# FFT mixing and a maxout FFN on one core: the first batch's start reordered, the stage-one pieces of later batches regrouped, and the last stores spread over three queues

## The chip, the cores and the metric

The kernel runs on one NeuronCore of one Trainium2 chip. The core has a matrix engine (TensorE; PE in the profile, PEld for its weight loads), three engines for elementwise work (VectorE, here DVE; ScalarE, ACT; GpSimd, POOL), and SyncE (SP), which here only starts transfers. ACT and POOL start transfers too; an engine's name with a q behind it (SPq, ACTq, POOLq) is the sequencer of that engine starting one. Time is microseconds (us) of one execution on the device; the time of a kernel is the median of its runs.

## The reference

The input x has 8 batches of 3072 tokens with 256 features. Each batch goes through a two-dimensional Fourier transform, of which the real part is kept, and then through a feed-forward layer that takes the largest of three products:

```python
X = np.fft.fft(x, axis=1)
X = np.fft.fft(X, axis=2)
t = X.real.reshape(8 * 3072, 256)
h = np.maximum(np.maximum(t @ w1, t @ w2), t @ w3)      # 256 -> 768
out = h @ w_out                                         # 768 -> 256
```

The weights are float32 in memory; the output is float32 of 24576 x 256.

## The kernel before, in words

**The algebra.** Because x is real, tokens k and 3072 - k of a batch are the sum and the difference of an even part tE and an odd part tO, so only 1536 columns of each are computed. The feature transform is folded into the weights: gE, gO and gD are products of the cosine and sine tables md and nmd with differences of the weights (w2 - w1 and w3 - w1), gw is the linear part through w_out. The maximum then is a ReLU of one difference (stmp, on ACT) and a maximum with the other (hp for token k, hm for its mirror token, on DVE).

**The token transform of a batch** (class `Mix`) is done in pieces, each a method with a letter:

- `s(0)` to `s(6)`: stage one. Two matmuls of the input xt with a small table `tab` go to the two halves of a PSUM tile; ACT (sometimes DVE) casts the result into the tile tb. `s(6)` is a small one, for the last row (line 374; the others are line 369).
- `y`: two stores of a part of tb to a scratch buffer db in memory (line 383). `z` loads db back transposed, as yb (line 390). Both are on SP's queue.
- `u`: POOL copies one column of xt to x0u (line 394). `x0`: two small matmuls on x0u (line 399); ACT casts the result to x0s (line 401). `c`: ACT copies x0s into a column of yb (line 404).
- `k(which, g)`: stage two. For a group g of 512 columns, six or so small matmuls of yb with the tables te_tab (which = 0, giving tE) or to_tab (which = 1, giving tO), line 411, and a cast out of PSUM, line 413. `k(1, g)` needs what `c` wrote; `k(0, g)` does not.

**The main loop** runs over 8 batches x 18 units: three blocks of 512 columns, and in each six slices jc of 128 of the 768 hidden features. `begin(g)` multiplies tE and tO with gE and gO (lines 436 and 437, or 771 and 772) and makes hp; `finish(g)`, one unit later, adds the product with gD (line 444) and makes hm. Every other unit from the seventh on is "split": POOL makes the sums plus and minus for it (line 764) from an even part (DVE, line 760) and an odd part (ACT, line 759). The second layer of a block (`l2_block`, lines 475, 483 and 460) is a generator of which ten steps are taken per unit of the following block. DVE writes its output tile ot (line 488), one half is stored by SP's queue (line 496), the other by an indirect store of POOL (line 570). The pool of ot has 6 buffers, the PSUM pool `ps_f` 3; the latter is shared by all the pieces above.

**What sets the order.** Every engine issues its instructions in the order in which the program text emits them. The pieces of the next batch are placed at units of the current one by tables: `ahead0` for what is done during batch 0, `ahead` during batches 1 to 6. A unit's pieces come after its `begin`, `finish` and ten second-layer steps. `turn` (line 129) puts ACT copies for the batch after next at units 5 to 12.

**The start.** For batch 0 all of this has to be done before the loop begins, on tables that are made at the same time: `table(0)`, `table(1)` and `table(2)` are three ACT instructions (te_tab, an absolute value, to_tab; lines 279, 281 and 283), called for the columns 0 to 512, and then for 512 to 1024, which only group g = 1 uses. `product` and `keep_product` make the first half of gE, gO and gD (PE line 296; casts in lines 306 and 308, line 309 for gD). `warm_up(n)` issues n matmuls on zeros (line 588) whose result nobody reads.

**The end.** The second layer of the last block is `l2_last`. It takes the four sub-blocks in the order 3, 0, 1, 2; each leaves its output tile through plain stores, six for the first and four for each of the others (line 531). For sub-block 2 the two halves of ot are copied out of PSUM separately (line 521), for the others in one copy (line 523).

Of the kernel before, what the change touches and what calls it, by code (L numbers as in the profile page):

```python
# [28 lines left out]
def _runs(slot):  # L29

    if slot == 11:
        return [(0, 48, 0), (48, 96, 16), (96, 128, 15 + 32 * 64)]
    t, u = divmod(slot, 3)
    edge, r = 96 - 32 * u, 4 * t + 1 + u
    return [(0, edge, r + 32 * 32 * u), (edge, 128, r + 1)]
# [15 lines left out]
def kernel(  # L51
# [9 lines left out]
    nc = tc.nc  # L61
# [78 lines left out]
    ps_s = ps_s_cm.__enter__()  # L140
# [86 lines left out]
    dve = nc.vector.tensor_copy  # L227
    half = gen.tile([128, 256], FP32, tag="half")
# [47 lines left out]
    def table(k, c0=1024, c1=NHALF + 1):  # L276
        cs = slice(c0, c1)
        if k == 0:
            nc.scalar.activation(out=te_tab[:, cs], in_=kvec[:, cs], func=AX.Sin, scale=step)
        elif k == 1:  # L280
            nc.scalar.activation(out=q[:, cs], in_=kvec[:, cs], func=AX.Abs)
        else:
            nc.scalar.activation(out=to_tab[:, cs], in_=q[:, cs], func=AX.Sin, scale=-step,
                                 bias=half_pi)

    def tables(c0, c1):
        for k in range(3):
            table(k, c0, c1)

    def product(i, half, jh, pool, tag):  # L290

        psg = pool.tile([128, 512], FP32, name="psg", tag=tag)
        hs = slice(half * 128, (half + 1) * 128)
        for k, (table, wt) in enumerate(((md, (w2_bf, w3_bf)[i]), (nmd, w1_bf))):
            for fc in range(2):
                nc.tensor.matmul(
                    psg[:, 0:384], table[fc][:, hs],
                    wt[:, fc * DFF + jh * 384: fc * DFF + jh * 384 + 384],
                    start=(k == 0 and fc == 0), stop=(k == 1 and fc == 1))
        return psg  # L300

    def keep_product(psg, i, half, jh, evict_e):

        cs = slice(jh * 384, (jh + 1) * 384)
        if half == 0:
            evict_e(out=gE[i][:, cs], in_=psg[:, 0:384])
        else:
            nc.scalar.copy(out=gO[i][:, cs], in_=psg[:, 0:384])
            nc.vector.tensor_scalar(out=gD[i][:, cs], in0=gO[i][:, cs], scalar1=dif,
                                    scalar2=None, op0=ALU.mult)  # L310
# [142 lines left out]
    def stored(st, mine, others):  # L453
        for group in others:
            tc.declare_no_dep(st.ins, group=group, reason="each store has rows of its own")
        tc.add_to_no_dep_group(mine, st.ins)

    def l2_hidden(po, hcols):
        for jc in range(NJC):
            nc.tensor.matmul(po, hcols(jc), wout_bf[:, jc * 256:(jc + 1) * 256],  # L460
                             start=False, stop=(jc == NJC - 1), skip_group_check=True)
            yield
# [36 lines left out]
    def l2_last(hp, hm, te, to, flipped):  # L499

        base = (B - 1) * S
        ter, tor = flipped
        for sub in (3, 0, 1, 2):
            slot = 8 + sub
            cp = slice(slot * 128, slot * 128 + 128)
            sp = slice(sub * 128, sub * 128 + 128)
            sm = slice((3 - sub) * 128, (4 - sub) * 128)
            ot = out_pool.tile([128, 512], FP32, name="ot", tag="ot")
            for (h, tev, tov, wo, hid) in (
                    (0, te[:, cp], to[:, cp], gw[:, 256:512], lambda jc: hp[:, jc, sp]),  # L510
                    (1, ter[:, sm], tor[:, sm], gw[:, 512:768], lambda jc: hm[:, jc, sm])):
                if h == 0 or sub == 2:
                    po = ps_o.tile([128, 512], FP32, name="po", tag="po")
                ph = po[:, h * 256:(h + 1) * 256]
                nc.tensor.matmul(ph, tev, gw[:, 0:256], start=True, stop=False)
                yield
                nc.tensor.matmul(ph, tov, wo, start=False, stop=True)
                yield
                yield from l2_hidden(ph, hid)
                if sub == 2:  # L520
                    nc.vector.tensor_copy(out=ot[:, h * 256:(h + 1) * 256], in_=ph)
            if sub != 2:
                nc.vector.tensor_copy(out=ot, in_=po)
            stores = [(p0, p1, base + k0, 0) for (p0, p1, k0) in _runs(slot)]
            for (p0, p1, k0) in _runs(slot):
                if k0 == 0:
                    p0, k0 = 1, 32
                stores.append((128 - p1, 128 - p0, base + S - k0 - 32 * (p1 - p0 - 1), 256))
            for k, (p0, p1, row, c) in enumerate(stores):
                eng = (nc.sync, nc.scalar)[k % 2]  # L530
                stored(eng.dma_start(out=out[row: row + 32 * (p1 - p0 - 1) + 1: 32, :],
                                     in_=ot[p0:p1, c:c + 256]), "direct", ("scattered",))

# [52 lines left out]
    def warm_up(n):  # L586
        for _ in range(n):
            nc.tensor.matmul(warm, zero[:, 0:128], zero, start=True, stop=True)
# [7 lines left out]
    m = Mix(0)  # L596
# [28 lines left out]
                                in_=moe_w_out.rearrange("(jc p) c -> p jc c", jc=NJC))  # L625
    for half in range(2):
        keep_product(product(0, half, 0, ps_f, "ps"), 0, half, 0, dve)
    for half in range(2):
        keep_product(product(1, half, 0, ps_s, "ps"), 1, half, 0, dve)
    tables(512, 1024)  # L630
    warm_up(6)
    m.c(0, 6, nc.scalar.copy)
    m.k(0, 0, dve)
    m.k(1, 0)

    rows_v = rows_f.rearrange("p (b r) -> p b r", r=12)
    adj = gen.tile([128, 12], FP32, tag="adj")
# [82 lines left out]
    for b in range(2, B):  # L720
# [3 lines left out]
        for ch in range(8):  # L724
# [1 line left out]
        at(b - 2, 13 + 3 * (b == 2), lambda b=b: mirror_first(b))  # L726

    ahead0 = {5: ("s0", "s1"), 6: ("s2", "y0", "s3"), 7: ("s4", "s5", "s6", "y1", "u"),
              8: ("z", "x"), 12: ("c",), 13: ("kO0",), 14: ("v0", "kE0", "kO1"),
              15: ("v1", "kE1"), 16: ("kO2",), 17: ("v2", "kE2", "end")}  # L730
    ahead = {1: ("s0", "s1"), 2: ("s2", "y0", "s3"), 3: ("u", "s4", "s5"), 4: ("s6", "y1", "x"),
             7: ("z",), 11: ("c",), 12: ("kO0",), 13: ("v0", "kE0", "kO1"), 14: ("v1", "kE1"),
             15: ("kO2",), 16: ("v2", "kE2", "end")}
    for b in range(B - 1):
# [56 lines left out]
    for g in range(B * UNITS):  # L791
        b, u = divmod(g, UNITS)
# [30 lines left out]
        if jc == NJC - 1:  # L823
            l2_some(1000)
            if g == B * UNITS - 1:
                finish(*prev)
            l2_queue.append(l2_last(hp, hm, mm.tE, mm.tO, flipped) if last else
                            l2_block(b, blk, hp, hm, mm.tE, mm.tO))
# [32 lines left out]
```

## Time and profile before

| what | value |
|---|---|
| median of 3 runs | 406.56 us (405.85 to 406.56) |
| the profiled execution | 405.21 us |
| its span, first to last instruction | 403.4 us |
| mean granted TensorE clock | 0.991 |
| PE busy | 383.7 us (95%) |
| DVE busy | 319.6 us (79%) |
| POOL busy | 322.1 us (80%) |
| ACT busy | 261.2 us (65%) |
| HBM traffic over the span | 173 GB/s |

The profile is of one execution. Start times in the rows are us from the span's start. A row of the timeline has start, duration, engine, line, operation, the tile written and the tiles read, shapes, how many instructions were merged into it, and in brackets how long the engine had been idle and what ended that. Matmuls are pipelined: a row's duration is longer than the distance to the next one, and what counts is the distance between starts. DMA-issuing rows tell how long the sequencer took to issue, not when the data arrived.

### The profile page before, as it was taken

Reading aid. Unit: us, or ns where it says so; the run is one execution under the profiler, and the core shown is the slowest. Engines: PE = TensorE matmul, PEld = TensorE weight load, DVE = VectorE, ACT = ScalarE, POOL = GpSimd, SP = SyncE. Lnnn points to the kernel's source line nnn. Section 1 sums busy time; section 2 is a strip of 40 time slices with the busy share of each in tenths; the row PEclk is TensorE's granted clock in tenths of the full one; section 3 lists DMA queues with packets and bytes.
Section 4 is the critical chain, followed back from the end, with each engine's and each line's share of the span. In section 5 each row is a group of like instructions: output and inputs, shape, how many; then the busy total and the mean of one; then the engine's idle time right before and its main releaser. Section 6 shows DMA issues by size and latency. Waiting matters only on the chain.

```text
span 403.4 us, 8304 instructions
## 1 busy us (share of the span) xinstructions
PE 383.7 (95%) x2695; PEld 236.7 (59%) x2743; DVE 319.6 (79%) x542; ACT 261.2 (65%) x466; POOL 322.1 (80%) x403
## 2 busy tenths in 40 slices
PE   7589899999999999999999999999999999999995
PEld 2245456656665566656665566656665566666574
DVE  7869887877887887877887887877887887887982
ACT  2565879768865778568875778568865546635430
POOL 7376279787988799897988799897988699788991
PEclk9799999999999999999999999999999999999999
DMA  8999968495765958394764958495532653322225
GB/s 122 196 187 174 176 180 158 118 169 131 178 141 121 185 147 166 109 178 116 192 149 109 190 146 160 115 160 143 149 107 78 149 141 100 94 70 67 89 81 142
DMA packets 69692, 56.30 MB, mean 140 GB/s; under 512 B 35040, under 2 KB 65248, under 8 KB 68452
## 3 DMA queue, kind: packets, MB, share of 16 engines
q0 software_dynamic: 23376, 26.27, 34.5%
q1 hardware_dynamic: 45106, 28.86, 27.6%
q10 hardware_dynamic: 1168, 0.65, 0.6%
q8 instruction: 21, 0.34, 0.3%
q14 instruction: 21, 0.17, 0.2%
HBM read 38.15 MB, written 31.71 MB: 173 GB/s over the span
## 4 chain that ended last, share of the span: by engine, by line
PE 73%; DMA 9%; DVE 5%; issue 5%; POOL 4%; ACT 3%; SPq 1%; ACTq 0%; DVEq 0%; POOLq 0%
PE po L460 25%; PE pse L444 10%; PE pse L436 7%; DMA out_dram<-ot 6%; PE pse L437 5%; PE pse L771 4%; PE po L483 4%; PE d L757 3%; PE pse L772 3%; PE e L755 3%; DVE even L760 3%; PE ps L411 2%; DMA xt<-in_x_dram 2%; PE pl L475 2%; POOL minus L764 2%
## 5 line engine op out<-in xcount | busy, mean ns | idle before, releaser
L450 ACT ACTIVATE stmp<-pse 128x512 bf16<-128x512 f32 x150 | 89.9, 600 | 62.1 <-PE pse L444 45.2
L764 POOL TENSOR_TENSOR plus<-even,odd 128x512 bf16<-128x512 f32 x69 | 87.9, 1274 | 39.8 <-DVE even L760 32.2
L570 POOL DMA_INDIRECT out_dram<-ot,rows_m x92 | 102.4, 1113 | 17.9 <-issue 8.3
L773 DVE SCALAR_TENSOR_TENSOR hp<-pse,plus 128x512 bf16<-128x512 f32 x69 | 47.6, 690 | 50.6 <-PE pse L772 21.1
L764 POOL TENSOR_TENSOR minus<-even,odd 128x512 bf16<-128x512 f32 x69 | 87.6, 1269 | 0.0
L460 PE MATMUL po<-wout_bf,hp 128*128 128x256 bf16 x576 | 86.1, 273 | 0.3
L460 PE MATMUL po<-wout_bf,hm 128*128 128x256 bf16 x576 | 78.6, 273 | 0.0
L444 PE MATMUL pse<-tO,gD 128*128 128x512 bf16 x218 | 70.8, 379 | 1.0 <-DVE hp L451 0.4
L460 PEld LDWEIGHTS <-hp 128*128 128x128 bf16 x576 | 56.4, 98 | 26.1
L460 PEld LDWEIGHTS <-hm 128*128 128x128 bf16 x576 | 56.4, 98 | 16.3
L488 DVE TENSOR_TENSOR ot<-po,even 128x512 f32<-128x512 f32 x92 | 62.9, 683 | 0.0
L451 DVE TENSOR_TENSOR hp<-pse,stmp 128x512 bf16<-128x512 f32 x75 | 51.5, 686 | 10.3 <-ACT stmp L450 8.7
L436 PE MATMUL pse<-tE,gE 128*128 128x512 bf16 x147 | 55.6, 378 | 1.6 <-ACT stmp L450 0.2
L451 DVE TENSOR_TENSOR hm<-pse,stmp 128x512 bf16<-128x512 f32 x75 | 51.7, 689 | 5.9 <-ACT stmp L450 2.1
L760 DVE SCALAR_TENSOR_TENSOR even<-vb,wcol,e 128x512 f32<-128x512 bf16 x69 | 51.0, 739 | 0.0
L437 PE MATMUL pse<-tO,gO 128*128 128x512 bf16 x130 | 49.2, 379 | 0.7 <-ACT tO L413 0.4
L785 DVE SCALAR_TENSOR_TENSOR hm<-pse,minus 128x512 bf16<-128x512 f32 x69 | 47.2, 684 | 1.8 <-PE pse L444 0.4
L759 ACT ACTIVATE odd<-d 128x512 f32<-128x512 f32 x69 | 41.3, 598 | 6.6
L129 ACT COPY xt<-xt 64x762 bf16<-64x762 bf16 (+1 forms) x48 | 40.2, 838 | 1.1
L372 ACT CAST tb<-ps 128x512 bf16<-128x512 f32 x46 | 24.8, 589 | 21.7 <-PE ps L369 21.7
L444 PEld LDWEIGHTS <-gD 128*128 128x128 bf16 x219 | 21.2, 97 | 23.2 <-issue 5.0
L483 PE MATMUL po<-gw,tO 128*128 128x512 bf16 x86 | 32.7, 380 | 0.0
(155 smaller groups left out, 462.4 us busy)
## 6 DMA issues: line engine op xcount, KB each, us to landing
yb<-db SPq DMA_DIRECT2D x7, 833.0 KB
xt<-in_x_dram POOLq DMA_DIRECT2D x14, 384.0 KB, 8.3
out_dram<-ot SPq DMA_DIRECT2D x56, 96.0 KB
out_dram<-ot SPq DMA_DIRECT2D x64, 64.0 KB
db<-tb SPq DMA_DIRECT2D x21, 192.0 KB
vb<-vd SPq DMA_DIRECT2D x23, 128.0 KB
xt<-in_x_dram POOLq DMA_DIRECT2D x7, 400.0 KB
xt<-in_x_dram POOLq DMA_DIRECT2D x7, 368.0 KB, 5.6
```

The costliest lines, as they stand in the source:

```text
L436: nc.tensor.matmul(pse[:, 0:n], gE[i][:, js], te, start=True, stop=False)
L437: nc.tensor.matmul(pse[:, 0:n], gO[i][:, js], to, start=False, stop=True)
L444: nc.tensor.matmul(pse, gD[i][:, js], to, start=False, stop=True, skip_group_check=True)
L450: nc.scalar.activation(out=stmp[:, 0:n], in_=pses[0][:, 0:n], func=AX.Relu)
L451: nc.vector.tensor_tensor(out=dst, in0=src3, in1=stmp[:, 0:n], op=ALU.max)
L460: nc.tensor.matmul(po, hcols(jc), wout_bf[:, jc * 256:(jc + 1) * 256], start=False, stop=(jc == NJC - 1), skip_group_check=True)
L483: nc.tensor.matmul(po, to[:, cp], gw[:, 256:768], start=True, stop=True)
L488: nc.vector.tensor_tensor(out=ot.rearrange("p (h c) -> p h c", h=2), in0=po.rearrange("p (h c) -> p h c", h=2), in1=lin.unsqueeze(1).to_br ...
L570: stored(nc.gpsimd.indirect_dma_start(out, bass.IndirectOffsetOnAxis(ap=rows_m[0:128 - lo, at_row: at_row + 1], axis=0), ot[lo:128, 256:51 ...
L760: nc.vector.scalar_tensor_tensor(out=even3, in0=vb, scalar=wcol[:, jc:jc + 1], in1=e3, op0=ALU.mult, op1=ALU.add)
L764: nc.gpsimd.tensor_tensor(out=dst, in0=even3, in1=odd3, op=op)
L773: nc.vector.scalar_tensor_tensor(out=dst, in0=pse2, scalar=0.0, in1=sums[g][0], op0=ALU.max, op1=ALU.max)
```

## The change

Three places are touched.

1. **The start.** Of the second set of tables, `table(0)` and `table(1)` are now emitted ahead of the last product, and `table(2)` after `k(1, 0)`. The fillers ahead of stage two go from 6 to 2. `k(0, 0)` is emitted ahead of the cast and gD of the last product. ACT's order there was: cast of gO, three tables, `c`, cast of tO. It becomes: two tables, cast of gO, `c`, cast of tO, the third table.
2. **Pieces ahead.** During batches 1 to 6, `s6` moves from unit 4 to unit 2, `y1` from unit 4 to unit 3, `u` behind `y1` in unit 3, and `x` (x0) from unit 4 to unit 5, so that unit 4 has none of them and stage one stands in three groups instead of four. During batch 0, `x` moves from unit 8 to unit 9.
3. **The last stores.** The 18 stores of `l2_last` went alternately over SP's and ACT's queues; they now go in turn over ACT's, SP's and POOL's, sub-block 2 beginning with SP's.

```diff
-                eng = (nc.sync, nc.scalar)[k % 2]
+                eng = (nc.scalar, nc.sync, nc.gpsimd)[(k + (sub == 2)) % 3]
...
-    for half in range(2):
-        keep_product(product(1, half, 0, ps_s, "ps"), 1, half, 0, dve)
-    tables(512, 1024)
-    warm_up(6)
+    keep_product(product(1, 0, 0, ps_s, "ps"), 1, 0, 0, dve)
+    table(0, 512, 1024)
+    table(1, 512, 1024)
+    psg = product(1, 1, 0, ps_s, "ps")
+    warm_up(2)
+    m.k(0, 0, dve)
+    keep_product(psg, 1, 1, 0, dve)
     m.c(0, 6, nc.scalar.copy)
-    m.k(0, 0, dve)
     m.k(1, 0)
+    table(2, 512, 1024)
...
     ahead0 = {5: ("s0", "s1"), 6: ("s2", "y0", "s3"), 7: ("s4", "s5", "s6", "y1", "u"),
-              8: ("z", "x"), 12: ("c",), 13: ("kO0",), 14: ("v0", "kE0", "kO1"),
+              8: ("z",), 9: ("x",), 12: ("c",), 13: ("kO0",), 14: ("v0", "kE0", "kO1"),
               15: ("v1", "kE1"), 16: ("kO2",), 17: ("v2", "kE2", "end")}
-    ahead = {1: ("s0", "s1"), 2: ("s2", "y0", "s3"), 3: ("u", "s4", "s5"), 4: ("s6", "y1", "x"),
+    ahead = {1: ("s0", "s1"), 2: ("s2", "y0", "s3", "s6"), 3: ("s4", "s5", "y1", "u"), 5: ("x",),
              7: ("z",), 11: ("c",), 12: ("kO0",), 13: ("v0", "kE0", "kO1"), 14: ("v1", "kE1"),
              15: ("kO2",), 16: ("v2", "kE2", "end")}
```

## The prediction

> **What bounds the kernel now.** I read the page's busy shares first, then busy time by stage, then PE's own waits, and only then the timeline at the three places of the change.
>
> ```profile
> PE 383.7 (95%) x2695; PEld 236.7 (59%) x2743; DVE 319.6 (79%) x542; ACT 261.2 (65%) x466; POOL 322.1 (80%) x403
> ```
>
> The second view is busy time by stage: window, length, then busy us of PE, PEld, DVE, ACT and POOL, the clock share, DMA share and GB/s.
>
> ```profile
> 10.74:14.15 3.41, 0.84 (x6) 0.25 (x6) 2.77 (x8) 1.28 (x3) 2.89 (x7) 1.00 1.27 195
> 15.00:17.00 2.00, 0.37 (x4) 0.24 (x2) 1.72 (x9) 1.34 (x4) 0.00 (x0) 0.50 1.24 245
> 20.98:24.39 3.41, 2.40 (x20) 1.37 (x20) 2.01 (x5) 2.35 (x5) 2.35 (x4) 1.00 0.78 195
> 136.00:181.50 45.50, 44.99 (x320) 27.93 (x324) 36.61 (x58) 33.20 (x59) 39.60 (x48) 1.00 0.69 151
> ```
>
> A middle batch takes 45.5 us with PE busy 44.99 and every other engine below 40: there only time that PE itself sheds counts. The start is different: from 20.98 to 24.39 PE is busy 2.40 of 3.41 us.
>
> ```profile
> PE psx L399 <- POOL x0u L394: 1.2, 6, 0.2
> ```
>
> That is PE's costliest wait (total, times, longest) that comes back batch after batch: six times 0.2 us for POOL's x0u.
>
> **The start.**
>
> ```profile
> 21.79 0.48 ACT L308 CAST gO<-psg 128x384 bf16<-128x384 f32 x1 [1.35 <-PE psg L296]
> 21.81 1.24 PE L588 MATMUL warm<-zero 128*128 128x512 bf16 x5
> 22.04 2.17 POOL L164 DMA_DIRECT2D w_bf<-in_moe_w_dram  x3 [7.40 <-DMA yb<-db]
> 22.17 0.63 ACT L279 ACTIVATE te_tab<-kvec 128x512 bf16<-128x512 f32 x1
> 23.32 0.69 DVE L413 CAST tE<-ps 128x512 bf16<-128x512 f32 x1 [0.50 <-PE ps L411]
> 23.35 0.72 ACT L283 ACTIVATE to_tab<-q,half_pi 128x512 bf16<-128x512 f32 x1
> 23.98 0.20 ACT L404 COPY yb<-x0s 98x6 bf16<-98x6 bf16 x1
> 24.67 0.59 ACT L413 CAST tO<-ps 128x512 bf16<-128x512 f32 x1 [0.49 <-PE ps L411]
> 25.31 0.38 PE L437 MATMUL pse<-tO,gO 128*128 128x512 bf16 x1 [0.45 <-ACT tO L413]
> 25.72 0.60 ACT L450 ACTIVATE stmp<-pse 128x512 bf16<-128x512 f32 x1 [0.46 <-PE pse L437]
> 28.36 0.49 PE L296 MATMUL psg<-w_bf,md_all 128*128 128x384 bf16 x2
> ```
>
> ACT idles 1.35 us before the last gO cast; two of the three tables (0.63 us for the first, the second starts the third at 23.35) fit into that gap, as their input is older than it. The cast stays at 21.79, and the copy into yb follows at about 22.2 instead of 23.98. The yb transfer it also needs has landed: POOL's weight loads, which wait for it, start at 22.04. Two fillers instead of six end near 22.0 (five in the row take 1.24 us), so the matmuls of k(0, 0) go at about 22.05 and tE's cast at 22.5, not 23.32; gD then follows tE on DVE, and its reader is finish(0), 2 us later. k(1, 0) starts when the copy ends (22.4) and tO's cast stands at 22.9, against 24.67. The first tO matmul then waits for tE instead (22.5 + 0.69, and a slot): 23.5 against 25.31. What is queued behind the moved table(2): the first stmp. ACT is free of it at 22.9 + 0.59 + 0.72 less their overlap, about 24.0, and the stmp's input is ready at 23.9, so it costs 0.1. The stmp comes about 1.7 us earlier.
>
> Late next is a load: the product at 28.36 reads the second half of the weights. The three loads are issued from 22.04, after the yb landing, and the change moves none of them. The page's DMA answer has one landing of the three:
>
> ```profile
> w_bf<-in_moe_w_dram POOLq DMA_DIRECT2D x3, 192.0 KB, 5.4
> ```
>
> The last is issued at about 23.5 and lands at 28.9, so the second, which this product needs, lands about a us earlier (192 KB at the 195 GB/s of the window from 20.98), say 27 to 27.9. PE would now arrive at 26.6. The gain there is between 0.5 us (27.9) and 1.7 us (no wait); I take 1.2, as the third transfer shares its time with loads behind it and so the second should be nearer 27.
>
> **The pieces ahead.**
>
> Unit 4 of a middle batch, on PE, from the last two second-layer matmuls to the next unit:
>
> ```profile
> 179.63 0.38 PE L460 MATMUL po<-wout_bf,hp 128*128 128x256 bf16 x2
> 179.95 0.24 PE L374 MATMUL ps<-xt,tab 128*64 128x128 bf16 x1
> 180.38 0.26 PE L399 MATMUL psx<-tabx,x0u 128*98 128x17 bf16 x2 [0.20 <-POOL x0u L394]
> 180.50 0.38 PE L771 MATMUL pse<-tE,gE 128*128 128x512 bf16 x1
> ```
>
> The two of line 460 take 0.11 us each from start to start, so they are through at 179.85, and the next unit begins at 180.50. The pair s6 and x0 costs 0.65 us, of which only 0.2 are a named wait; the rest is PE draining between small matmuls of two kinds. Batch 0 has x0 by itself:
>
> ```profile
> 53.45 0.22 PE L399 MATMUL psx<-tabx,x0u 128*98 128x17 bf16 x2
> 53.52 0.38 PE L771 MATMUL pse<-tE,gE 128*128 128x512 bf16 x1
> ```
>
> That is 0.07. It also has s6 at the end of a group, and a middle batch has the group that s6 joins:
>
> ```profile
> 51.12 0.22 PE L374 MATMUL ps<-xt,tab 128*64 128x128 bf16 x1 [0.46 <-ACT tb L372]
> 51.27 0.39 PE L444 MATMUL pse<-tO,gD 128*128 128x512 bf16 x1
> ...
> 174.08 0.62 PE L369 MATMUL ps<-xt,tab 128*64 128x512 bf16 x4
> 174.63 0.39 PE L771 MATMUL pse<-tE,gE 128*128 128x512 bf16 x1
> ```
>
> s6 takes 0.15, of which the way out of the group, about 0.09, is paid anyway (the four at 174.08 take 0.55; two slots of a 512-column matmul, 0.215 each, and one of 0.12 for the way out make that up): 0.06. Saved are 0.65 - 0.07 - 0.06 = 0.52 us in each of six batches, 3.1 us. I take 2.8, since s6's cast now stands on ACT right behind those of s2 and s3, ahead of the next unit's stmp and of DVE's work on it:
>
> ```profile
> 171.69 1.07 ACT L372 CAST tb<-ps 128x512 bf16<-128x512 f32 x2 [0.77 <-PE ps L369]
> 174.52 1.07 ACT L372 CAST tb<-ps 128x512 bf16<-128x512 f32 x2 [1.25 <-PE ps L369]
> ```
>
> Bounds: 3.1 above; below, s6 becomes the third stage-one tile in a row, and at 51.12 such a third one waited 0.46 for ACT's cast to free a buffer. Then 0.06 a batch is left, 0.4 us.
>
> At no cost I count: y1 on SP a unit earlier (its issuing now stands ahead of a unit's stores: rival b); u, whose copy is still done two units before its reader; x0s, needed only in unit 11, though ACT's cast of it now stands behind a turn copy; and x one unit later in batch 0, which waited for nothing.
>
> **The last stores.**
>
> ```profile
> 397.61 2.83 SPq L531 DMA_DIRECT2D out_dram<-ot  x4
> 398.57 0.42 DVE L521 COPY ot<-po 128x256 f32<-128x256 f32 x1 [0.52 <-PE po L460]
> 398.78 2.11 ACTq L531 DMA_DIRECT2D out_dram<-ot  x4
> SPq L531 <- DMA out_dram<-ot: 2.0, 2, 1.0
> L531 ACTq DMA_DIRECT2D out_dram<-ot x2: 531/544/556, 399.7 to 400.3; - x2
> out_dram<-ot,rows_m POOLq DMA_INDIRECT x4, 2.6
> ```
>
> The last copy ends at 398.99, the last issue (the fourth of ACT's four) begins at 400.3 and ends at 400.89, the span ends 2.5 us after that. The queues do not start when their tiles are ready: SP waits twice, 2.0 us in all, for an earlier store's landing, and ACT begins its four only at 398.78, though sub-block 1 had been copied a us and more before, as SP's first of the four, of the same tile, shows at 397.61. With three queues ACT and SP have three of the last eight stores each and POOL two. The third on ACT or SP begins at about 399.6 to 399.7, one issue (0.54) and its gap before 400.3: 0.7 us. POOL's second goes out at about 398.3, and with the 2.6 us of its indirect stores lands near 400.9, not last. Bounds: 1.3 us if the landing waits go too (the third then begins right behind the copy, at 399.0); a loss if POOL's store takes the 5.4 us of its loads above: it would land at 403.7, later than the span of before ends, and with some 1 us to close the kernel (an estimate) cost 1.3.
>
> The Trainium skill, "DMA: Bandwidth & Descriptors", section "Issuing engines are not separate DMA queues", says that starting transfers from several engines saves only the sequencer's issue time, since all run on the same 16 DMA engines. By it this part would be worth the one issue, 0.54 us, and the sum 0.2 us less than mine; the waits for landings would stay, and the rows here cannot separate the two.
>
> **The sum.** 1.2 + 2.8 + 0.7 = 4.7 us. The profiled execution took 405.21 us (span 403.4 and 1.8 around it), which gives 400.5. It lies 1.35 under the median of the runs; from 406.56 the sum is 401.9.
>
> **The rivals.** (a) s6 waits for a buffer in every batch: 406.56 - 1.2 - 0.4 - 0.7 = 404.3. For it speaks the 0.46 at 51.12. Against it, in batch 0 the plan has k(0, 2) and end in the same unit just ahead of the three; in unit 2 of a middle batch ACT is through with s0 and s1 by 172.76, 1.3 us before s2 starts, so three buffers should be free. (b) The other side: SP's queue. y1's two issues now stand ahead of unit 4's stores, and if these land later by as much, DVE waits for an ot buffer and PE for DVE. The first row is y1's issuing, the second a piece of the chain in this stretch.
>
> ```profile
> 181.73 1.34 SPq L383 DMA_DIRECT2D db<-tb  x2
> ...
> 172.59 4.17 DMA out_dram<-ot
> ```
>
> So a store's landing does stand in the chain there. The rival decides once the delay passes the 0.47 us saved per batch: at 1.34 the loss is 0.87 x 6 = 5.2, and 406.56 - 1.9 + 5.2 = 409.9. Against it, PE has no wait on DVE in a middle batch, and the pool has six buffers. (c) With four fillers less, the clock falls. It stands at 0.50 from 15 to 17 us, after PE had been busy 0.84 of 3.41 us from 10.74 to 14.15. A half clock for two such windows, 6.8 us, would cost up to 3.4 us with PE full: 406.56 - 4.7 + 3.4 = 405.3, and without the start's gain 406.5, no change. Against it, the moved matmuls fill what the fillers leave, so PE's 2.40 of 3.41 us should grow. The Trainium skill, "TensorE: Matmul & The Clock Gate", Part 1, has it that the gate watches a free-running window of about 3.4 us and halves the clock after an idle one. By that rule too, no window here is idle enough.
>
> **How the numbers follow.** The forecast has 0.56 (own range 400.5 to 403.7: 0.5 to 1.7 at the start, 2.4 to 3.1, or 0.4 to 0.52 a batch, between, 0 to 1.3 at the end), a still larger gain 0.04, (a) 0.20, (c) 0.08, (b) 0.12. A change of 0.2%, 0.8 us, is about what a measurement of this kernel can tell from none. Faster: 0.56 + 0.04 + 0.20 and half of (c), 0.84; same: 0.04; slower: 0.12. The range takes in the forecast's bounds, (a) and the milder (c): 399.9 to 405.4; (b), the harder (c) and the tails stay out.
>
> **What would show it.** In the profile after: ACT's line 404 copy near 22.2 and the first stmp near 24.0; line 296's second half waiting for a load near 27; no wait of PE for x0u, a middle batch of 45.0 us instead of 45.5, s6 adding 0.06 to its group; the last issue of line 531 at PE's end + 1.1 us. Wrong if s6 shows a wait on line 372, if SP's line 496 falls behind, if the clock share falls below 1.00 after 21 us, or if POOL's stores land last.

## The result and the profile after

The changed kernel took 402.4 us (median of 6 runs, 401.85 to 403.36), the kernel before beside it 406.04 (405.48 to 406.56): a ratio of 0.9914, with a 95% interval of 0.9898 to 0.9930, or 3.5 us (2.8 to 4.1) gained. The forecast was 401.9 and 4.7 us gained. The profiled execution of the changed kernel took 403.04 us with a span of 400.8, so it lies 0.6 us above its median, while the one of before lay 1.35 under its own. Times of profile rows are therefore compared stage by stage below, and gains by the ratios. The fences show rows chosen from the view that is named; rows between them are left out.

The page's row of PE, after:

```profile
PE 381.5 (95%) x2691; PEld 236.9 (59%) x2739; DVE 319.2 (80%) x542; ACT 260.2 (65%) x466; POOL 324.6 (81%) x408
```

**The middle batches.** The timeline of DVE has the copies that open the outputs of a batch. Two of them, one batch apart, first before and then after:

```profile
142.31 0.69 DVE L488 TENSOR_TENSOR ot<-po,even 128x512 f32<-128x512 f32 x1
187.79 0.68 DVE L488 TENSOR_TENSOR ot<-po,even 128x512 f32<-128x512 f32 x1
```

```profile
141.38 0.69 DVE L488 TENSOR_TENSOR ot<-po,even 128x512 f32<-128x512 f32 x1
186.27 0.68 DVE L488 TENSOR_TENSOR ot<-po,even 128x512 f32<-128x512 f32 x1
```

From one of these rows to the next, a batch takes 44.89 us instead of 45.48, 0.59 less. PE's timeline after has the two places, s6 behind its group and x0 by itself:

```profile
173.53 0.22 PE L374 MATMUL ps<-xt,tab 128*64 128x128 bf16 x1
173.68 0.39 PE L774 MATMUL pse<-tE,gE 128*128 128x512 bf16 x1
...
181.29 0.22 PE L399 MATMUL psx<-tabx,x0u 128*98 128x17 bf16 x2
181.36 0.38 PE L444 MATMUL pse<-tO,gD 128*128 128x512 bf16 x1
```

Neither has a wait in brackets: s6 is followed 0.15 us later by the unit, x0 0.07 later. The six waits for x0u are gone from PE's list.

**The start.** Of PE's new waits after, two of 0.4 us or more are for transfers:

```profile
PE psg L296 <- DMA w_bf<-in_moe_w_dram: 1.0, 1, 1.0
PE ps L411 <- DMA yb<-db: 0.4, 1, 0.4
```

and the timeline of the start reads

```profile
22.78 0.47 ACT L308 CAST gO<-psg 128x384 bf16<-128x384 f32 x1
23.38 0.22 ACT L404 COPY yb<-x0s 98x6 bf16<-98x6 bf16 x1
23.57 2.18 POOL L164 DMA_DIRECT2D w_bf<-in_moe_w_dram  x3 [7.54 <-DMA yb<-db]
25.22 0.60 ACT L450 ACTIVATE stmp<-pse 128x512 bf16<-128x512 f32 x1
29.04 0.50 PE L296 MATMUL psg<-w_bf,md_all 128*128 128x384 bf16 x2 [1.02 <-DMA w_bf<-in_moe_w_dram]
```

From the cast of gO to the first stmp it is 2.44 us, against 3.93 before (21.79 to 25.72): 1.5 us shorter. But this execution was late, by about 1 us at the cast, since its x arrived later (DVE's first copy of it starts at 9.65 instead of 7.75), and then PE waits 1.02 us for the weights' second half. The first outputs of batch 0 are 0.17 us later than in the profile of before.

**The end.** The last rows of DVE, the issues of line 531, and the instructions that close the kernel (durations in ns: shortest, median, longest; then the start of the first and the last), after:

```profile
395.61 0.43 DVE L521 COPY ot<-po 128x256 f32<-128x256 f32 x1 [0.52 <-PE po L460]
L531 ACTq DMA_DIRECT2D out_dram<-ot x7: 375/432/530, 391.0 to 396.1; - x7
L531 SPq DMA_DIRECT2D out_dram<-ot x6: 314/371/539, 391.0 to 396.5; - x6
L531 POOL DMA_DIRECT2D out_dram<-ot x5: 501/537/572, 391.6 to 395.4; - x5
L859 POOLq DRAIN  x3: 46/103/4654, 395.4 to 400.5; - x3
L859 SPq DRAIN  x3: 7/7/7, 399.0 to 400.3; - x3
```

and the last two of these before, where the last copy ended at 398.99:

```profile
L856 POOLq DRAIN  x3: 46/97/5237, 393.4 to 403.1; - x3
L856 SPq DRAIN  x3: 7/7/7, 402.6 to 402.9; - x3
```

The last store on SP or ACT goes out at 396.5, 0.45 us behind the last copy, where it was 1.3 us before. SP's first DRAIN, which follows its waits for the stores' landings, starts at 399.0, 2.9 us behind the copy, where it was 3.6. So far the stores are as forecast. But POOL's DRAIN, 4.65 us long, starts at 395.4 together with POOL's last store and ends at 400.0, a microsecond after SP is through, and the last barrier follows it. Before it ended at 398.6, four microseconds ahead of SP. From the last copy to the end of the span it is 4.77 us, against 4.40 before: 0.37 us lost where 0.7 were to be gained. A second loss lies outside the span, where no row shows it: the device time is 1.8 us longer than the span in the profiled execution of before, and 2.24 to 2.26 us longer in the six runs of the changed kernel.

### The profile page after: what moved, and what is told of

Same layout as the page of the kernel before. It is cut to its first block, busy times and chain, and to the rows that moved or that the text cites. A ratio compares the mean times of both kernels' runs of the same rounds, so it can differ in the third digit from the quotient of the medians.

```text
span 400.8 us, 8295 instructions
## 1 busy us (share of the span) xinstructions
PE 381.5 (95%) x2691; PEld 236.9 (59%) x2739; DVE 319.2 (80%) x542; ACT 260.2 (65%) x466; POOL 324.6 (81%) x408
## 4 chain that ended last, share of the span: by engine, by line
PE 81%; DMA 8%; DVE 4%; ACT 3%; issue 2%; SPq 1%; POOL 0%; DVEq 0%; POOLq 0%; ACTq 0%
PE po L460 29%; PE pse L444 11%; PE pse L436 8%; PE pse L437 6%; PE po L483 4%; PE pse L774 4%; PE d L760 3%; PE e L758 3%; PE pse L775 3%; DMA yb<-db 3%; PE ps L369 3%; PE ps L411 2%; PE pl L475 2%; DMA xt<-in_x_dram 2%; ACT tb L372 2%
## 5 line engine op out<-in xcount | busy, mean ns | idle before, releaser
L444 PEld LDWEIGHTS <-gD 128*128 128x128 bf16 x219 | 21.4, 98 | 23.1 <-issue 5.0
```

What stands on the lines that cost most here:

```text
L444: nc.tensor.matmul(pse, gD[i][:, js], to, start=False, stop=True, skip_group_check=True)
```

## The experiments

Twelve runs follow: eleven kernels, each a few lines away from the kernel before or the changed one, and the changed kernel once more. Ratios are against the kernel before on the same chip, whose median was 405.7 to 405.9.

### One part at a time

The start alone, on the kernel before:

```diff
-    for half in range(2):
-        keep_product(product(1, half, 0, ps_s, "ps"), 1, half, 0, dve)
-    tables(512, 1024)
-    warm_up(6)
+    keep_product(product(1, 0, 0, ps_s, "ps"), 1, 0, 0, dve)
+    table(0, 512, 1024)
+    table(1, 512, 1024)
+    psg = product(1, 1, 0, ps_s, "ps")
+    warm_up(2)
+    m.k(0, 0, dve)
+    keep_product(psg, 1, 1, 0, dve)
     m.c(0, 6, nc.scalar.copy)
-    m.k(0, 0, dve)
     m.k(1, 0)
+    table(2, 512, 1024)
```

> The kernel before with the first part of the change alone: two tables of the second set ahead of the last product, table(2) behind k(1, 0), two fillers for six. My theory now: the first stmp comes 1.5 us earlier against the cast of the last gO than before, and PE then waits about 1 us at line 296 for the weights' second half, so that 0.5 to 1 us is left: 405.0 to 405.6 where before is 406.0. The prediction's own term was 1.2 (404.8). Rival: the fillers were needed and the start gains nothing or loses (406.0 or more, and a clock share under 1.00 after 21 us).

404.9 us, ratio 0.9979 (0.9967 to 0.9991): 0.85 us (0.4 to 1.3). Its timeline:

```profile
21.76 0.48 ACT L308 CAST gO<-psg 128x384 bf16<-128x384 f32 x1 [0.56 <-PE psg L296]
22.14 0.22 ACT L404 COPY yb<-x0s 98x6 bf16<-98x6 bf16 x1
23.96 0.59 ACT L450 ACTIVATE stmp<-pse 128x512 bf16<-128x512 f32 x1
26.67 0.50 PE L296 MATMUL psg<-w_bf,md_all 128*128 128x384 bf16 x2
...
32.72 1.56 POOL L129 COPY xt<-xt 64x1651 bf16<-64x1651 bf16 x1 [2.21 <-DMA xt<-in_x_dram]
33.19 1.38 DVE L203 TENSOR_SCALAR kvec<-kvec,s_of,phi 128x513 f32<-128x513 f32 x1
34.60 1.70 DVE L203 TENSOR_SCALAR q<-kvec 128x513 f32<-128x513 f32 x1
```

Up to the product of line 296 this is the prediction, time for time: the copy at 22.14 (22.2 there), the first stmp at 23.96 (24.0), the product at 26.67 (26.6). The wait of about 1 us for the weights that was expected before this run did not come in its profile. The gain there is 1.7 us. At the first outputs it is 1.19, and 1.12 at the last copy. The half microsecond between is lost around 34 us, where DVE's first operation of line 203 takes 1.38 us; before it took 0.88. More on that below.

The pieces alone, on the kernel before:

```diff
-              8: ("z", "x"), 12: ("c",), 13: ("kO0",), 14: ("v0", "kE0", "kO1"),
+              8: ("z",), 9: ("x",), 12: ("c",), 13: ("kO0",), 14: ("v0", "kE0", "kO1"),
...
-    ahead = {1: ("s0", "s1"), 2: ("s2", "y0", "s3"), 3: ("u", "s4", "s5"), 4: ("s6", "y1", "x"),
+    ahead = {1: ("s0", "s1"), 2: ("s2", "y0", "s3", "s6"), 3: ("s4", "s5", "y1", "u"), 5: ("x",),
```

> The kernel before with the second part alone: the pieces of later batches regrouped. My theory: each of six batches is 0.52 us shorter, 3.1 us in all (402.9 where before is 406.0), the last copy of ot 3.1 us earlier, and the time from it to the span's end as before, 4.4 us. The prediction's term was 2.8. Rival: part of the 3 us that the two profiles show between batch 1 and batch 7 comes from the changed start, which moved batch 0 against its loads; then this run gains less than 2.5.

403.11 us, ratio 0.9931 (0.9914 to 0.9949): 2.8 us (2.1 to 3.5). In its profile a batch takes 44.89 us, and from the first outputs to the last it gains 3.4 us; the profiled execution is the fastest of the six, 1.7 us under their median. No middle batch waits for a buffer of stage one, and no wait of DVE or PE has come in place of the one removed.

The stores alone, on the kernel before:

```diff
-                eng = (nc.sync, nc.scalar)[k % 2]
+                eng = (nc.scalar, nc.sync, nc.gpsimd)[(k + (sub == 2)) % 3]
```

> The kernel before with the third part alone: the last stores over ACT, SP and POOL in turn. My theory: it loses. POOL's closing DRAIN ends about 4.1 us after POOL's last DMA issue (398.6 after an issue that ended at 394.5 in the profile before, 400.0 after 395.9 in the one after), and with POOL's last store 3.0 us after the last copy of another sub-block's tile this is later than SP's last landing. From the last copy of ot to the end 4.8 us instead of 4.4: 406.4 where before is 406.0. The prediction's term was a gain of 0.7 (405.3).

406.54 us, ratio 1.0021 (1.0006 to 1.0036): this part by itself makes the kernel slower, by 0.85 us (0.2 to 1.5). The closing rows:

```profile
L856 POOLq DRAIN  x3: 46/102/4654, 398.8 to 404.0; - x3
L856 SPq DRAIN  x3: 7/7/7, 402.4 to 403.8; - x3
```

POOL's DRAIN ends at 398.8 + 4.65 = 403.5, 1.1 us after SP is through, and the stretch from the last copy to the end of the span is again 4.77 us. The three parts' medians add to 0.85 + 2.8 - 0.85 = 2.8 us, the lower end of the interval of the whole (2.8 to 4.1); the parts' own intervals leave room for its 3.5.

### The end: what the drain costs

The changed kernel, with POOL given stores of the first two sub-blocks (3 and 0) only:

```diff
-                eng = (nc.scalar, nc.sync, nc.gpsimd)[(k + (sub == 2)) % 3]
+                eng = ((nc.scalar, nc.sync, nc.gpsimd)[k % 3] if sub in (3, 0)
+                       else (nc.sync, nc.scalar)[k % 2])
```

> The changed kernel, but POOL takes stores of sub-blocks 3 and 0 alone; those of 1 and 2 go over SP and ACT in turn. My theory: POOL's last issue ends 2.4 us earlier, its DRAIN ends before SP's last landing wait, and the time from the last copy of ot to the end falls from 4.8 to between 4.0 and 4.4 us: 0.4 to 0.8 us under the changed kernel, 401.6 to 402.0. Rival: the DRAIN is long for another reason (the landings of all queues); then it ends as late as in the changed kernel and nothing is gained.

401.84 us, ratio 0.9902 (0.9879 to 0.9926). The closing rows:

```profile
L860 POOLq DRAIN  x3: 46/103/5707, 394.9 to 401.7; - x3
L860 SPq DRAIN  x3: 7/7/7, 401.2 to 401.5; - x3
```

The DRAIN is even longer, 5.7 us, but it ends at 400.6, ahead of SP, as the theory has it and not its rival. The end stretch is 4.11 us.

The changed kernel with the stores of before, on SP and ACT in turn:

```diff
-                eng = (nc.scalar, nc.sync, nc.gpsimd)[(k + (sub == 2)) % 3]
+                eng = (nc.sync, nc.scalar)[k % 2]
```

> The changed kernel with the last block's stores on SP and ACT in turn, as before the change: the beginning and the pieces stay. Theory (GpSimd's closing drain): without a late store on GpSimd, its drain ends well ahead of SP's last wait, and the stretch from the last copy of L523 to the end of the span is the 4.4 us of before or a little less, against 4.77 with the three queues; the time is 0.3 to 0.5 us below the changed kernel on the same chip. Rival (GpSimd's queue isn't what costs; the tail differs by chance from run to run): the stretch stays at 4.7 or more, or the time equals the changed kernel's within 0.2.

401.48 us, ratio 0.9896 (0.9878 to 0.9914); the end stretch is 4.64 us, between the 4.4 of the theory and the 4.7 of its rival. The changed kernel once more, on the same chip:

> The changed kernel once more, beside the three others on the same chip: 402.4 us, 0.9914 of the kernel before, with the drain of GpSimd ending last and a tail of 4.7 to 4.8 us. Its start should lie where that run's transfers of x land: if the profiled run before it was late by 1 to 1.5 us only by chance, the copy of L404 stands near 22.2 here and the wait at L296 is 1 us or longer.

402.04 us, ratio 0.9920 (0.9895 to 0.9944). The two intervals overlap, so the times by themselves do not part theory and rival; the profiles do. Over all profiles the stretch from the last copy to the end of the span falls into three groups, by who has the late stores:

| last stores | end stretch, us | device time outside the span, us |
|---|---|---|
| three queues to the end (six profiles) | 4.77 in each | 2.19 to 2.32 (42 runs) |
| SP and ACT alone (five profiles) | 4.40 to 4.72 | 1.77 to 1.90 (87 runs) |
| POOL in the first two sub-blocks only (three profiles) | 4.11 to 4.22 | 1.76 to 2.13 (17 runs) |

With three queues it is the same to 0.01 us in every profile, as it is set by one instruction of one engine. With SP and ACT alone it moves with the landings. So three queues cost 0.05 to 0.37 us inside the span, and by the medians of the last column (2.25 and 1.84) 0.4 outside it, together 0.5 to 0.8: this is the size of the 0.85 that the stores alone lost. What that time outside the span is, no row shows. POOL early gains 0.2 to 0.6 inside the span and gives up to 0.3 of it back outside, and its time is not better than that of the kernel without POOL (ratios of 0.9902 and 0.9896). The profile of before, with 4.40, had the shortest end stretch of its kind.

### The pieces: what the 0.5 us were

The kernel before with s6 moved and nothing else:

```diff
-    ahead = {1: ("s0", "s1"), 2: ("s2", "y0", "s3"), 3: ("u", "s4", "s5"), 4: ("s6", "y1", "x"),
+    ahead = {1: ("s0", "s1"), 2: ("s2", "y0", "s3", "s6"), 3: ("u", "s4", "s5"), 4: ("y1", "x"),
```

> The kernel before with s6 moved to unit 2 of a later batch and nothing else; y1 and x stay in unit 4. If s6 costs 0.06 in its new group and x by itself 0.07, with the 0.2 of the wait for x0u left in unit 4 as it was, the shift is 0.3 us per batch (0.52 less 0.2), 1.9 in all and 404.2 us; if without s6 in front u's copy is no nearer and the draining stays, nothing is gained. If u's copy is through by then, since x stands in a later place of the queue without s6, the whole 0.52.

406.31 us, ratio 1.0010 (0.9996 to 1.0024): nothing gained. In its profile, which is of the slowest of twelve runs, the same batch takes 45.61 us, 0.13 more than before. The place in unit 4, and the row of PE's waits:

```profile
180.66 0.38 PE L460 MATMUL po<-wout_bf,hp 128*128 128x256 bf16 x2
181.19 0.26 POOL L394 COPY x0u<-xt 128x49 bf16<-128x49 bf16 x1
181.50 0.26 PE L399 MATMUL psx<-tabx,x0u 128*98 128x17 bf16 x2 [0.46 <-POOL x0u L394]
181.62 0.38 PE L771 MATMUL pse<-tE,gE 128*128 128x512 bf16 x1
...
PE psx L399 <- POOL x0u L394: 2.8, 6, 0.5
```

The copy that x0 needs on POOL, and the one before the change, in the first kernel's profile:

```profile
180.07 0.26 POOL L394 COPY x0u<-xt 128x49 bf16<-128x49 bf16 x1
```

In both, x0 starts 0.05 us behind the end of POOL's copy (181.45, and 180.33 with x0 at 180.38). With s6 away, PE comes earlier and waits longer: from 2 x 0.11 us behind 180.66 to the next unit at 181.62 it is 0.74 us, where the pair cost 0.65. So s6 had been lying under the wait for x0u. Per batch that is 0.09 lost there, and the rest of the 0.13 agrees with the 0.06 that s6 was to cost in its new group. What carries the gain must then be the other half of the edit: x0 a unit later, behind a copy that is long done (in the changed kernel it ends at 179.5, and x0 starts at 181.3). x0 moved by itself was not run, so this is concluded and not shown alone.

### The start: three costs behind the gain

The changed kernel with the first product of the weights' second half one unit later:

```diff
-                    (1, lambda: m.k(1, 1)), (1, lambda: next(second)), (1, lambda: next(first)),
-                    (2, lambda: m.v(1)),
+                    (1, lambda: m.k(1, 1)), (1, lambda: next(second)),
+                    (2, lambda: m.v(1)), (2, lambda: next(first)),
```

> The changed kernel with the first of the four products that read the second half of the weights issued in unit 2 instead of unit 1. Theory (the weights' landing takes back part of the gain at the start): PE no longer waits 1.0 us at L296 near 29, the four products follow one another in unit 2, and batch 0's shift behind them is 0.5 to 1.0 us better; the time is that much below the changed kernel on the same chip. Rival (the wait only moves: unit 3, whose first layer reads these products, waits for the casts of L306 and L308 instead): PE shows a wait for gE, gO or gD near 31 of about the same length, and the time is equal or up to 0.5 us longer.

401.57 us, ratio 0.9918 (0.9888 to 0.9949). PE's wait for the weights is gone from the list, but 0.65 us are lost between the fifth and the seventh stmp, where four products now stand together ahead of unit 3: as the rival has it, if not by all of the gain. From the first stmp to the ninth 0.25 us are lost against before, and 0.32 in the repeat of the changed kernel, where PE waited only 0.15 us for the weights (1.19 in the first profile of the changed kernel, with the wait of 1.02). The 0.5 to 1.0 us of the theory don't show in the time: the interval does not tell it from zero against the changed kernel on the same chip.

The changed kernel with six fillers:

```diff
-    warm_up(2)
+    warm_up(6)
```

> The changed kernel with the six fillers of before in place of two, the tables in the changed order. Theory (ACT's order carries the start's gain and the transfer of yb now bounds it): four fillers of 0.22 us lie in front of the matmuls of k(0, 0) and cost 0 where yb lands after 22.9 us and up to 0.9 where it lands at 22.0; the time is 0 to 0.7 us above the changed kernel. Rival (the fewer fillers carry the gain): the first stmp falls back by all of 0.9 or more. The granted clock is 1.00 after 21 us in both cases.

402.6 us, ratio 0.9910 (0.9894 to 0.9927). Its start:

```profile
22.46 1.87 PE L588 MATMUL warm<-zero 128*128 128x512 bf16 x6
23.24 0.22 ACT L404 COPY yb<-x0s 98x6 bf16<-98x6 bf16 x1
23.43 2.17 POOL L164 DMA_DIRECT2D w_bf<-in_moe_w_dram  x3 [8.51 <-DMA yb<-db]
24.17 0.39 PE L411 MATMUL ps<-te_tab,yb 98*128 98x96 bf16 x6
25.98 0.60 ACT L450 ACTIVATE stmp<-pse 128x512 bf16<-128x512 f32 x1
```

yb is there at 23.4, but the fillers hold PE until 24.17, and the first stmp stands 2.55 us behind the weights' issue, where it is 1.65 with two fillers (25.22 less 23.57 above): 0.9 us for four fillers. The theory had them free where yb lands late, so its number fell, and the rival's 0.9 is there. Half of it is the clock: the fillers start at 22.46, and until about 23.3 the clock was at one half. Windows of 1 us, the clock share third from the end:

```profile
22.00:23.00 1.00, 1.00 (x5) 0.41 (x3) 0.06 (x1) 0.29 (x1) 0.00 (x0) 0.50 0.72 286
23.00:24.00 1.00, 1.00 (x6) 0.38 (x5) 0.00 (x0) 0.41 (x2) 0.57 (x1) 0.86 0.75 214
```

By the length of their row about two fillers went through in those 0.8 us. At 0.215 us each, as before, all six would have been through at about 23.75 (an estimate), still 0.3 us behind yb. So the fewer fillers carry a part of the gain at the first stmp, up to 0.9 us. In the time of the whole kernel the ratio is that of the changed kernel (0.9914 and 0.9920): a loss of 0.9 us is about as wide as its interval and isn't seen there.

**What the landing of yb decides.** In the profiles of the changed start with two fillers, the first stmp follows the issue of the weights, which itself waits for yb's landing, at 1.65 us, in one case 1.92. In the four with the old start ACT's copy of line 404 came 1.3 to 2.0 us after yb had landed, behind its tables, and did not wait for it. So the old start had that much slack towards yb, and the new one has little or none. Over the profiles of the changed start yb landed between 22.0 and 23.6 us, and with two fillers the first stmp stands 0.5 to 1.8 us earlier than in the profile of before, accordingly. The rest of batch 0 varies more: its first outputs lie between 1.4 us earlier and 1.5 us later than in the profile of before, so that the start's gain rests on the twelve runs of the start alone, and not on any one profile.

**What DVE and POOL do to each other.** The half microsecond lost near 34 us in the first experiment has a cause that shows in every profile. POOL copies x of batch 1 (line 129) when it has landed, and DVE works on the angles of the last tables (line 203, kvec and q, then q again) at about that time. Two profiles of kernels with the same code there, first the repeat of the changed kernel, then the kernel that puts two edits together, further below:

```profile
34.28 0.54 DVE L203 TENSOR_SCALAR kvec<-kvec,s_of,phi 128x513 f32<-128x513 f32 x1
34.41 1.83 POOL L129 COPY xt<-xt 64x1651 bf16<-64x1651 bf16 x1 [2.79 <-DMA xt<-in_x_dram]
34.86 1.67 DVE L203 TENSOR_SCALAR q<-kvec 128x513 f32<-128x513 f32 x1
```

```profile
35.30 1.93 DVE L203 TENSOR_SCALAR kvec<-kvec,s_of,phi 128x513 f32<-128x513 f32 x1
35.39 1.56 POOL L129 COPY xt<-xt 64x1651 bf16<-64x1651 bf16 x1 [3.36 <-DMA xt<-in_x_dram]
37.27 1.70 DVE L203 TENSOR_SCALAR q<-kvec 128x513 f32<-128x513 f32 x1
```

One of the first two operations takes 0.54 us (0.43 for q) when no copy runs, and up to 1.93 when one does: in each such pair it ends 0.3 us behind the end of POOL's copy (36.53 and 36.24, 37.23 and 36.95). The sum of the three operations is 3.03 us in the profile of before (0.88, 1.70, 0.45). Where it is more or less, batch 0 gets later or earlier there by the same amount:

| kernel | sum, us | against before | shift of batch 0 over that stretch |
|---|---|---|---|
| start alone | 3.53 | +0.50 | +0.50 |
| pieces alone | 2.62 | -0.41 | -0.37 |
| stores alone | 3.11 | +0.08 | +0.10 |
| s6 alone | 3.56 | +0.53 | +0.53 |
| stores of before | 3.86 | +0.83 | +0.84 |
| repeat of the change | 2.62 | -0.41 | -0.37 |
| POOL early | 3.96 | +0.93 | +0.95 |
| six fillers | 4.06 | +1.03 | +1.04 |
| two edits together | 4.06 | +1.03 | +1.05 |

(The stretch is from the ninth to the eleventh stmp, 36 to 39 us in the profile of before. In two further profiles with these operations in their old place, the first of the changed kernel and that of the later product, it is the third operation that meets the second copy; their sums are 0.6 lower than before, and batch 0 is 0.5 earlier behind it.)

So the three operations take between 0.6 us less and 1.0 us more than in the profile of before, and batch 0 shifts with them. Which it is goes with the moment at which x of batch 1 lands, against the moment at which DVE gets there, in kernels with and without the change. The Trainium skill, "SBUF — State Buffer", section "Who interferes with whom", names a mechanism that fits: VectorE and GpSimd share a pair of ports to the SBUF, a tensor_scalar in a mode that takes both ports and a GpSimd operation exclude each other for a whole instruction, and whoever comes first holds the other up. The rows agree: the operation gets through only behind the copy, and a copy that comes second, as at 34.41 in the first pair, takes 1.83 us instead of 1.56.

The changed kernel with the first two of these operations in unit 1:

```diff
-                    (1, lambda: m.k(1, 1)), (1, lambda: next(second)), (1, lambda: next(first)),
+                    (1, lambda: m.k(1, 1)), (1, lambda: next(second)), (1, lambda: angle(0)), (1, lambda: next(first)),
...
-                    (3, lambda: m.k(0, 1)), (3, lambda: angle(0)),
+                    (3, lambda: m.k(0, 1)),
```

> The changed kernel with angle(0), the two DVE operations of L203 on kvec and q, in unit 1 instead of unit 3. Theory (GpSimd's copies of L129 hold up DVE's operations of L203 on SBUF when both run at once, and so eat a part of the start's gain): the two take 0.54 and 0.43 us instead of up to 1.93 and 1.70, no matrix multiply near 37 us waits 0.9 us or more for DVE's hp, and the first twelve stmp of batch 0 stand 0.3 to 1.0 us earlier against the first one than in the changed kernel. The later q of L203, still in unit 4, may go on waiting for the second copy (1.4 us). Rival (these operations are long because DVE itself is slowed, wherever they stand): they take 1.7 us in unit 1 as well.

401.6 us, ratio 0.9902 (0.9875 to 0.9928). Its rows:

```profile
27.75 0.54 DVE L203 TENSOR_SCALAR kvec<-kvec,s_of,phi 128x513 f32<-128x513 f32 x1
28.32 0.43 DVE L203 TENSOR_SCALAR q<-kvec 128x513 f32<-128x513 f32 x1
...
36.49 1.45 POOL L129 COPY xt<-xt 64x1524 bf16<-64x1524 bf16 x1
36.61 1.62 DVE L203 TENSOR_SCALAR q<-q 128x513 f32<-128x513 f32 x1
```

Away from the copy the two take 0.54 and 0.43 us, so they are not long by themselves: the theory holds and its rival falls. But the third, left where it was, now meets the second copy and takes 1.62 us instead of 0.45. The collision has moved. From the first stmp to the twelfth 0.35 us are lost against before, where the two profiles of the changed kernel lose 0.68 and gain 0.09: the 0.3 to 1.0 us hoped for do not stand out of that spread, nor in the time.

### Putting the edits together

POOL early and the later product, with the two edits shown above:

> GpSimd given stores of the first two sub-blocks only, and the first product of the second weight half in unit 2. If the drain and the weights' landing are two separate costs, the gains add: 0.4 to 0.6 us of the one and 0.5 to 1.0 of the other below the changed kernel, 401.0 to 401.5 us. If the product only moves its wait, the time is the 401.8 of the stores' edit by itself.

And to these the earlier angle, here in unit 2 ahead of the last product:

```diff
-                    (2, lambda: next(first)), (2, lambda: next(first)), (2, lambda: next(first)),
-                    (3, lambda: m.k(0, 1)), (3, lambda: angle(0)),
+                    (2, lambda: next(first)), (2, lambda: next(first)),
+                    (2, lambda: angle(0)), (2, lambda: next(first)),
+                    (3, lambda: m.k(0, 1)),
```

> GpSimd given stores of the first two sub-blocks only, the first product of the second weight half in unit 2, and angle(0) in unit 2 ahead of the last product. If the three costs are separate, 0.4 to 1.0 us below the 400.6 of the first two together: 399.6 to 400.2 us. If the earlier angle delays the casts that unit 3 reads by as much (0.97 us of DVE), the time stays at 400.6.

The two edits together: 400.58 us, ratio 0.9873 (0.9853 to 0.9893), below the 401.0 to 401.5 expected. All three: 400.63 us, ratio 0.9865 (0.9845 to 0.9885), the time that was expected if the earlier angle gains nothing. Both are faster than the kernel before, and than the changed kernel too: the first by an interval that ends just below that of the changed kernel on the same chip (0.9895 to 0.9944), the second by one that lies below both intervals of the changed kernel, though on another chip. The earlier angle adds nothing that can be told from zero; the third operation takes 1.5 us there too. The end stretch is 4.22 and 4.15 us. Why the two gain together what neither showed clearly alone is not shown: the profile of the two edits is of a slow execution (403.52 us) in which PE waits 0.5 us for the weights all the same, at 31.4.

## Why the prediction was right, and where it was not

The time, 402.4, lies 0.5 us from the forecast of 401.9 and inside its narrower range. That it is so close is in part luck. The forecast went from a median before of 406.56; beside the result it was 406.04, from which the same sum gives 401.3. The gain was 3.5 us (2.8 to 4.1) and not 4.7. Of the three terms, 1.2 + 2.8 + 0.7, the middle one holds, the first is smaller and the last has the wrong sign.

**The start, 1.2 forecast, 0.85 (0.4 to 1.3) measured alone.** The steps on ACT hold, to 0.1 us in the profile of the start alone: cast, copy, tO, first stmp. "Late next is a load" holds in some executions: in four profiles of the changed start PE stands 0.5 to 1.2 us at line 296 for the weights, in the others, that of the start alone among them, 0.2 or less. Two things were not in the working. "The yb transfer it also needs has landed" was read from one execution, in which yb was 1.9 us ahead of ACT's copy; with the copy moved forward by 1.8 that slack was gone, and in six of the eight other profiles with two fillers the copy or PE waits for yb, by 0.1 to 1.5 us. And the gain had to pass the place where DVE and POOL collide, whose rows (0.88 and 1.70 us for operations that take 0.54 and 0.43 elsewhere) stood in the trace of before. That place took 0.5 of the 1.7 us in the profile of the start alone.

**The pieces, 2.8 forecast, 2.8 (2.1 to 3.5) measured alone.** Batch by batch it is 0.59 us where the working has 0.52: 3.1 to 3.5 us from the first outputs to the last in nine profiles that have this part, 2.6 in the tenth. The reason for taking 2.8, s6's cast ahead of the next stmp, does not show: unit 3 follows 0.15 us behind s6, as it did in the row forecast. What varies lies near 290 us, where ACT waits for a later batch's yb, 1.0 us in the changed kernel's profile and 1.5 in the one with 2.6; it waits there in the profile of the start alone too (0.7), so not for the pieces. What fell is the explanation: "only 0.2 are a named wait; the rest is PE draining between small matmuls of two kinds". Up to x0's start it was the wait for POOL's copy of x0u, with s6 lying under it, as the experiment with s6 alone shows. The sum came out since both edits were made at once; in that the term was lucky.

**The last stores, 0.7 gained forecast, a loss measured.** This is the step that failed: POOL's second store "lands near 400.9, not last". It did not land last: the trace's packets of POOL's queue end at 397.2 in the profile after, those of SP's and ACT's at 398.1. But POOL's DRAIN behind it is what ends last, 4.1 us after the issue of its last store, and it was in no term. Its row stood in the profile of before, 5.2 us long and covered by SP. Nor does the "1.8 around it" hold: with the last stores on three queues it is 2.25. The part that was forecast, queues that issue earlier, came: 0.9 us earlier by the last issue, 0.6 by SP's last wait; it lies hidden behind the drain. By the rule of the Trainium skill, "DMA: Bandwidth & Descriptors", section "Issuing engines are not separate DMA queues", which the prediction weighed, the part was to be worth 0.54 us; the drain leaves neither that nor the 0.7.

**The rivals.** (a) No middle batch waits for a PSUM buffer ahead of s6; the one wait of 0.5 us, in batch 0, is there as before. (b) DVE has one wait for an earlier store, 1.1 us in the last block, after as before, and none in the middle batches. (c) The clock: half speed lasts to 21.0 us before and, by the shares of the 1 us windows, to 21.4 and 22.0 in the two profiles of the changed kernel, but it begins ahead of the fillers, and with six of them it lasted to 23.3. With the old start it ended between 20.3 and 22.6. It varies from execution to execution, and fewer fillers do not bring it. The bound "1.00 after 21 us" was drawn too tight from one execution. The prediction's "no window here is idle enough" does not hold either: in two profiles, that of the two edits and that of six fillers, the clock went to one half once more for 3.4 us, from 40.8 and from 40.4, behind 3.41 us of which PE had been busy 1.97 and 1.99. This cost next to nothing: batch 0's shift was 1.49 and 1.29 us ahead of it and 1.47 and 1.37 behind.

## What to carry to other kernels

A slack read from one execution (a transfer that "has landed") belongs to that execution: when its reader is moved forward, the gain is at most the slack, and other executions may have less of it. A forecast of a time leans on the median it starts from, so the gain has to be compared as well. A queue that is given work at the very end has to be closed as well, so the last instruction of each engine belongs in the sum, covered or not. Where several small pieces stand in front of one wait, only the piece that waits is worth moving: take another one away, and the wait grows in its place.

## What the hardware showed

- POOL's DRAIN at the kernel's end took 4.65 to 6.2 us in the fourteen profiles, and ended 4.1 to 5.2 us after POOL's last issue of a store, about 2.8 us after the last packet of its queue in the profile after. What it waits for, the trace does not show.
- With the last stores on three queues, POOL's among them, the device time was 2.19 to 2.32 us longer than the span in 42 runs, with them on SP and ACT alone 1.77 to 1.90 in 87. What the 0.4 us are, the trace does not show.
- A DVE operation on the SBUF of 0.43 to 0.54 us takes up to 1.93 us when one of POOL's copies runs (1.45 to 1.56 us by itself); the sum of three such operations gives the shift of batch 0 to 0.04 us in the nine kernels of the table.
- The transfer of yb, read back from DRAM by four loads, of which batch 0's first group needs three: POOL's issues that wait for it started 2.2 to 2.5 us after the issue of the third in nine profiles and 3.2 to 3.6 us in five, with nothing in between. What parts them stays open. All four of the old start are among the nine, which with so few is no evidence that the change makes it later.
